# Attention with a threshold, then a maxout FFN: heads taken four at a time, and the product with v turned round

## The chip, the cores and the metric

The kernel runs on one core of one Trainium2 chip. Its time is the device time in microseconds (us); the number that counts is the median of several runs. A profiled execution of the same program gives the trace.

## The reference

For each of 8 batches and 8 heads (576 positions, 64 features a head) the scores are thresholded near the row maximum, softmaxed and multiplied with v. The heads are laid side by side to x, of 4608 rows and 512 columns, and x goes through a maxout FFN.

```python
scores = scale * np.matmul(q, k.transpose(0, 1, 3, 2))
thresh = np.max(scores, axis=-1, keepdims=True) - tau
scores = np.where(scores >= thresh, scores, -1000000000.0)
scores = scores - np.max(scores, axis=-1, keepdims=True)
attn = np.exp(scores)
attn = attn / (np.sum(attn, axis=-1, keepdims=True) + 1e-09)
x = np.matmul(attn, v)               # then heads side by side: 4608 x 512
h = np.maximum(np.maximum(x @ w1, x @ w2), x @ w3)     # 4608 x 768
out = h @ w_out
```

## The kernel before, in words

The work goes over 32 pairs of heads (8 batches, 4 pairs each). A pair is cut into 5 units of query rows: four units hold 128 rows of each of the two heads, the fifth holds the last 64 rows of both heads, stacked. A *tile* below is one 128x576 block of scores; a pair has 9 of them, a batch 36.

In a unit (`unit`), `scores` makes each tile with matmuls on half of the array: keys are split in two halves j of 288, which lie on partitions 0 to 63 and 64 to 127, so q is loaded twice, once for each half. VectorE takes the row maximum (L164). In units 0 to 2 ScalarE then makes a steep Prelu (L173) and an Exp of both heads at once (L175). In units 3 and 4 it makes one Exp (L167), and VectorE masks by comparing with a threshold (L168). P, in bf16, goes through a DMA transpose (L177) to pt. Two units later `pv_unit` multiplies: pt is the stationary operand, v with a column of ones the moving one, so the row sum comes as column 65 of the output o. `normalize` divides into X, whose rows are positions; `x_transposed` turns X by five more DMA transposes (L218) into xt. `prep` turns q and k by TensorE for the next pair, after unit 2.

The FFN of a batch is a list of 18 pieces, `todo`: the transposes of X, 12 `hid` (6 blocks of columns f by 2 parts a of the rows, 3 weights each, maximum taken by ScalarE's copy and two VectorE passes) and 5 `outp`. One piece is issued per unit, beside the attention of the next batch; the last batch's pieces follow at the end. Loads, P transposes and X transposes share SP's queue in order; v and the outputs go by POOL's queue. The engines' final order is set by the tile framework's scheduler, which may move instructions of one engine past each other where nothing forbids it.

PSUM has 8 banks: 4 for scores (two tiles), 2 for o, 2 for transposes and FFN.

Of the kernel before, what the change touches and what calls it, by code (L numbers as in the profile page):

```python
# [11 lines left out]
F32 = mybir.dt.float32  # L12
# [22 lines left out]
):  # L37
    nc = tc.nc
# [14 lines left out]


    wts = []
    for i, w in enumerate((moe_w1, moe_w2, moe_w3)):
        t = one.tile([128, 4, DF], BF16, name=f"w{i}")
        for ko in range(4):
            nc.gpsimd.dma_start(out=t[:, ko, :], in_=w[ko * 128:(ko + 1) * 128, :])
        wts.append(t)  # L60
    wo = one.tile([128, 6, DM], BF16, name="wo")
    for ko in range(6):
        nc.gpsimd.dma_start(out=wo[:, ko, :], in_=moe_w_out[ko * 128:(ko + 1) * 128, :])


    NPB = 4
    p_ring = [one.tile([128, 2, KP], BF16, name=f"pring{i}") for i in range(NPB)]
    for t in p_ring:
        nc.vector.memset(t[:, :, S:], 0.0)
    NVB = 3  # L70
    v_ring = [one.tile([128, 2, NK, D + 1], BF16, name=f"vring{i}") for i in range(NVB)]
    for t in v_ring:
        nc.vector.memset(t[:, :, :, D:], 1.0)
# [13 lines left out]
    def load(b, hp):  # L87
        h0 = 2 * hp
        qm = ld.tile([128, 2, 4, 2, D], F32, name="qm")
        ql = ld.tile([128, 2, D], F32, name="ql")  # L90
        kk = ld.tile([128, 2, 2, 2, D], F32, name="kk")
        kl = ld.tile([32, 2, 2, D], F32, name="kl")
        vt = v_ring[(b * NP + hp) % NVB]
        for i in range(2):
            h = h0 + i
            for j in range(2):
                nc.sync.dma_start(out=qm[:, i, :, j, :],
                                  in_=q[b, h, 0:512, :].rearrange("(c p) d -> p c d", p=128))
                nc.sync.dma_start(out=ql[i * 64:(i + 1) * 64, j, :], in_=q[b, h, 512:S, :])  # L99
                nc.sync.dma_start(  # L100
                    out=kk[:, i, :, j, :],
                    in_=k[b, h, j * HS:j * HS + 256, :].rearrange("(c p) d -> p c d", p=128))
            nc.sync.dma_start(
                out=kl[:, i],
                in_=k[b, h].rearrange("(j u) d -> u j d", j=2)[256:HS])
            nc.gpsimd.dma_start(out=vt[:, i, 0:4, 0:D], in_=v[b, h, 0:512, :].rearrange("(c p) d -> p c d", p=128))  # L106
            nc.gpsimd.dma_start(out=vt[0:64, i, 4, 0:D], in_=v[b, h, 512:S, :])
        return dict(b=b, hp=hp, qm=qm, ql=ql, kk=kk, kl=kl, vt=vt)

    def prep(L):  # L110

        qt = qk.tile([128, 2, 512], F32, name="qt")
        qtl = qk.tile([128, 128], F32, name="qtl")
        kt = qk.tile([128, 2, HS], F32, name="kt")
        for i in range(2):
            tp = ps_f.tile([128, 512], F32, name="tp", tag="f")
            for c in range(4):
                nc.tensor.transpose(  # L118
                    tp[:, c * 128:(c + 1) * 128],
                    L["qm"][:, i, c].rearrange("p t d -> p (t d)"),  # L120
                    identf)
            nc.scalar.activation(out=qt[:, i], in_=tp, func=AF.Copy, scale=scale)  # L122
            tk = ps_f.tile([128, 512], F32, name="tk", tag="f")
            for c in range(2):
                nc.tensor.transpose(tk[:, c * 128:(c + 1) * 128],  # L125
                                    L["kk"][:, i, c].rearrange("p j d -> p (j d)"), identf)
            nc.tensor.transpose(tk[:, 256:HS], L["kl"][:, i].rearrange("p j d -> p (j d)"), identf[:32, :32])
            if i == 1:
                nc.tensor.transpose(tk[:, 384:512], L["ql"].rearrange("p t d -> p (t d)"), identf)
                nc.vector.tensor_scalar(out=qtl, in0=tk[:, 384:512], scalar1=scale, scalar2=None, op0=OP.mult)  # L130
            nc.vector.tensor_copy(out=kt[:, i], in_=tk[:, :HS])
        L.update(qt=qt, qtl=qtl, kt=kt)
# [207 lines left out]
```

## Time and profile before

| | |
|---|---|
| median of 3 runs | 829.45 us (828.59 to 839.41) |
| the profiled execution's own time | 821.5 us |
| its span, first to last instruction | 819.7 us |
| mean granted TensorE clock | 0.872 |
| busy: TensorE (PE) | 709.2 us, 87% |
| busy: VectorE (DVE) / ScalarE (ACT) / GpSimd (POOL) | 467.7 / 410.8 / 116.6 us |
| DMA: packets, bytes | 371429, 98.49 MB |

Busy time of PE counts overlapped matmuls once and changes with the granted clock, which is 1.00 at 2.4 GHz and 0.50 at 1.2 GHz. A busy share is an average over stages that differ; the windows and the timeline tell the stages apart. The profiled execution took 0.99 of the median.

### The profile page before, as it was taken

Reading aid. Unit: us, or ns where it says so; the run is one execution under the profiler, and the core shown is the slowest. Engines: PE = TensorE matmul, PEld = TensorE weight load, DVE = VectorE, ACT = ScalarE, POOL = GpSimd, SP = SyncE. Lnnn points to the kernel's source line nnn. Section 1 sums busy time; section 2 is a strip of 40 time slices with the busy share of each in tenths; the row PEclk is TensorE's granted clock in tenths of the full one; section 3 lists DMA queues with packets and bytes.
Section 4 is the critical chain, followed back from the end, with each engine's and each line's share of the span. In section 5 each row is a group of like instructions: output and inputs, shape, how many; then the busy total and the mean of one; then the engine's idle time right before and its main releaser. Section 6 shows DMA issues by size and latency. Waiting matters only on the chain.

```text
span 819.7 us, 14313 instructions
## 1 busy us (share of the span) xinstructions
PE 709.2 (87%) x5313; PEld 427.4 (52%) x5328; DVE 467.7 (57%) x1063; ACT 410.8 (50%) x585; POOL 116.6 (14%) x192
## 2 busy tenths in 40 slices
PE   0778799987999978998899988999799997999777
PEld 0445446653566545664466644665346654666354
DVE  0467645764467645775546754675446765577432
ACT  0556534555445654566535664455545555356512
POOL 5311111101111201112101121111111121010101
PEclk9977757998589987999679995899959997899979
DMA  9989884668666667668846786676866678554611
GB/s 169 154 150 145 146 128 75 114 120 148 107 108 108 140 138 130 113 111 167 134 84 115 120 169 109 108 109 132 147 119 92 109 152 146 118 82 78 126 30 58
DMA packets 371429, 98.49 MB, mean 120 GB/s; under 512 B 366752, under 2 KB 369056, under 8 KB 371360
## 3 DMA queue, kind: packets, MB, share of 16 engines
q1 hardware_dynamic: 326912, 80.27, 53.3%
q0 software_dynamic: 44448, 17.31, 15.3%
q8 instruction: 42, 0.69, 0.3%
q14 instruction: 27, 0.22, 0.1%
HBM read 44.04 MB, written 9.44 MB: 65 GB/s over the span
## 4 chain that ended last, share of the span: by engine, by line
PE 40%; issue 25%; DMA 24%; DVE 4%; SPq 3%; ACT 2%; POOL 1%; POOLq 0%; ACTq 0%; DVEq 0%
DMA pt<-pring 15%; PE ps L140 11%; PE o L193 8%; PE ph L242 5%; PE tp L118 3%; PE po L263 3%; PE ps L146 3%; PE ph L244 3%; DMA kk<-in_k_dram 3%; DMA vring<-in_v_dram 3%; PE tk L125 2%; DMA xt<-X 2%; DVE nm L164 2%; DMA qm<-in_q_dram 1%; SPq L99 1%
## 5 line engine op out<-in xcount | busy, mean ns | idle before, releaser
L164 DVE TENSOR_REDUCE nm<-ps 128x1 f32<-128x576 f32 x288 | 216.7, 754 | 120.8 <-PE ps L140 114.4
L140 PE MATMUL ps<-kt,qt 64*128 64x288 f32 x1024 | 226.1, 502 | 5.2 <-ACT z L167 2.5
L173 ACT ACTIVATE z<-ps,bm 128x576 f32<-128x576 f32 x192 | 141.9, 739 | 110.2 <-DVE bm L172 104.0
L193 PE MATMUL o<-vring,pt 128*128 128x65 bf16 (+3 forms) x1600 | 140.2, 209 | 64.8 <-DMA pt<-pring 59.8
L193 PEld LDWEIGHTS <-pt 128*128 128x128 bf16 (+3 forms) x1600 | 98.1, 106 | 160.5 <-DMA pt<-pring 96.2
L140 PEld LDWEIGHTS ps<-kt,qt 64*128 64x128 f32 x1024 | 105.0, 211 | 60.1 <-issue 20.3
L175 ACT ACTIVATE pring<-z 128x1152 bf16<-128x1152 f32 x96 | 111.5, 1162 | 2.4
L106 POOL DMA_DIRECT2D vring<-in_v_dram x64 | 50.5, 790 | 430.6 <-PE o L193 423.9
L167 ACT ACTIVATE z<-ps,nm 128x576 f32<-128x576 f32 x96 | 70.8, 738 | 72.3 <-DVE nm L164 72.2
L249 ACT ACTIVATE hm<-ph 128x256 bf16<-128x256 f32 x96 | 39.2, 409 | 135.0 <-PE ph L246 72.1
L244 PE MATMUL ph<-xt,w 128*128 128x256 bf16 x576 | 100.1, 287 | 1.1
L242 PE MATMUL ph<-xt,w 128*128 128x256 bf16 x576 | 89.6, 299 | 11.4 <-DMA xt<-X 9.3
L251 DVE TENSOR_TENSOR hm<-ph,hm 128x256 bf16<-128x256 f32 x96 | 44.0, 458 | 87.9 <-PE ph L246 46.1
L246 PE MATMUL ph<-xt,w 128*128 128x64 bf16 x576 | 91.4, 199 | 0.7 <-DMA xt<-X 0.7
L168 DVE SCALAR_TENSOR_TENSOR pring<-z 128x576 bf16<-128x576 f32 x96 | 71.6, 752 | 14.7 <-ACT z L167 13.8
L242 PEld LDWEIGHTS <-w 128*128 128x128 bf16 x576 | 55.8, 105 | 41.2 <-DMA xt<-X 14.2
L122 ACT ACTIVATE qt<-tp 128x512 f32<-128x512 f32 x64 | 38.1, 595 | 63.9 <-PE tp L118 62.7
L244 PEld LDWEIGHTS <-w 128*128 128x128 bf16 x576 | 59.0, 102 | 20.0 <-issue 9.1
L118 PE MATMUL tp<-identf,qm 128*128 128x128 f32 x256 | 48.0, 316 | 17.6 <-DMA qm<-in_q_dram 17.6
L263 PE MATMUL po<-wo,hT 128*128 128x512 bf16 (+1 forms) x225 | 60.1, 395 | 0.8
L246 PEld LDWEIGHTS <-w 128*128 128x128 bf16 x576 | 58.2, 101 | 4.5 <-issue 2.4
L267 POOL DMA_DIRECT2D out_dram<-ob x40 | 22.5, 563 | 261.1 <-ACT ob L266 261.1
(30 smaller groups left out, 436.5 us busy)
## 6 DMA issues: line engine op xcount, KB each, us to landing
qm<-in_q_dram SPq DMA_DIRECT2D x128, 128.0 KB, 2.6
kk<-in_k_dram SPq DMA_DIRECT2D x128, 64.0 KB, 2.2
out_dram<-ob POOLq DMA_DIRECT2D x32, 256.0 KB, 2.8
vring<-in_v_dram POOLq DMA_DIRECT2D x64, 64.0 KB, 4.0
pt<-pring SPq DMA_TRANSPOSE x160, 3.5
w<-in_moe_w_dram POOLq DMA_DIRECT2D x12, 192.0 KB, 8.5
ql<-in_q_dram SPq DMA_DIRECT2D x128, 16.0 KB, 2.2
kl<-in_k_dram SPq DMA_DIRECT2D x64, 16.0 KB, 2.1
```

What stands on the lines that cost most here:

```text
L118: nc.tensor.transpose(tp[:, c * 128:(c + 1) * 128], L["qm"][:, i, c].rearrange("p t d -> p (t d)"), identf)
L140: nc.tensor.matmul(ps[:, j, :HS], L["qt"][r, i, c * 128:(c + 1) * 128], L["kt"][r, i, :], start=True, stop=True)
L164: nc.vector.tensor_reduce(out=nm, in_=pv, axis=mybir.AxisListType.XY, op=OP.max, negate=True)
L167: nc.scalar.activation(out=zi, in_=pv, func=AF.Exp, bias=nm)
L168: nc.vector.scalar_tensor_tensor(out=P[:, i, :S], in0=z[:, i], scalar=thr, in1=z[:, i], op0=OP.is_ge, op1=OP.mult)
L173: nc.scalar.activation(out=zi, in_=pv, func=AF.Prelu, bias=bm, alpha=-STEEP)
L175: nc.scalar.activation(out=P[:, 0:n, :S], in_=z[:, 0:n], func=AF.Exp)
L193: nc.tensor.matmul(dst, pt[:kr, blk + m, cols], L["vt"][:kr, i, m, :], start=(m == 0), stop=(m == NK - 1))
L242: nc.tensor.matmul(pt[:, 0:256], w, st["xt"][:, 0:2, kc, :], start=(kc == 0), stop=(kc == 3))
L244: nc.tensor.matmul(pt[:, 0:256], w, st["xt"][:, 2:4, kc, :], start=(kc == 0), stop=(kc == 3), skip_group_check=True)
L246: nc.tensor.matmul(pt[:, 256:320], w, st["xt"][:, 4, kc, :64], start=False, stop=(kc == 3), skip_group_check=True)
L263: nc.tensor.matmul(po[:r, :], st["hT"][:, f, c * 128:c * 128 + r], wo[:, f, :], start=(f == 0), stop=(f == 5))
```

## The change

Heads are taken four at a time (a *quad*, 16 in all), in 9 steps `idx` of two tiles each. Step 0 to 3 hold the first two heads, 5 to 8 the other two, step 4 the last 64 rows of all four.

- q and k are loaded once, two heads side by side, with 1 KB runs (`(p c) d`: four consecutive rows a partition). `transposed` turns a pair by 5 transposes into one tile; `qs` is a copy of q^T with its two halves of partitions swapped, by two DMAs from SBUF to SBUF on POOL's queue. Key columns are split 256 and 320.
- v is loaded in f32 by SP's queue and cast by POOL (`cast_v`).
- `softmax` does two tiles with one `bm`; the Exp is one instruction a tile and, like the masking pass, also gives the row sum (`accum_out`) into `sm`. Masked steps are 1, 4 and 7. P is 1152 wide and one DMA transpose turns it.
- `product`: v is now stationary (64 columns, a head on each half of the array's columns), pt moves, so the output is x^T at once. X, its transposes and `normalize` are gone.
- `sums`: reciprocals of the row sums are transposed, written to DRAM and read back on 64 partitions each, so `product`'s output is multiplied by rows of `rb`.
- The FFN has 17 pieces, one a step; its row parts are two of 288.
- PSUM: three slots of two banks for scores, transposes and the product, two banks for the FFN. `side` places `sums` of the quad before at step 0, its `product` at 3 and 4, and the transposes for the next quad at 5 to 8.

```diff
-    ps_s = ctx.enter_context(tc.tile_pool(name="ps_s", bufs=2, space=PSUM))
-    ps_o = ctx.enter_context(tc.tile_pool(name="ps_o", bufs=1, space=PSUM))
+    ps_s = ctx.enter_context(tc.tile_pool(name="ps_s", bufs=3, space=PSUM))
     ps_f = ctx.enter_context(tc.tile_pool(name="ps_f", bufs=2, space=PSUM))
...
+            nc.sync.dma_start(out=m, in_=src[b, h, 0:512, :].rearrange("h (p c) d -> p h c d", c=4))
+            nc.sync.dma_start(out=r, in_=src[b, h, 512:S, :].rearrange("h p d -> p h d"))
...
+    def cast_v(L):
+        vb = vp.tile([128, 4, 4, D], BF16, name="vb")
+        vrb = vp.tile([128, 2, D], BF16, name="vrb")
+        nc.gpsimd.tensor_copy(out=vb, in_=L["vm"])
+        nc.gpsimd.tensor_copy(out=vrb, in_=L["vr"])
...
+    def transposed(L, n, pr):
+        m, r = L[n + "m"], L[n + "r"]
+        ps = slot("tp")
+        h0, h1 = 2 * pr, 2 * pr + 1
+        col = 192
+        for src in (m[:, h1, 0:2], m[:, h1, 2:4], r[:, h0:h0 + 2], m[:, h0, 0:2], m[:, h0, 2:4]):
+            np_ = src.shape[0]
+            nc.tensor.transpose(ps[:, col:col + np_], src.rearrange("p a d -> p (a d)"), identf[:np_, :np_])
+            col += np_
+        t = qk.tile([128, S], F32, name=n + "t")
+        if n == "q":
+            nc.scalar.activation(out=t, in_=ps[:, 192:768], func=AF.Copy, scale=scale)
+            s = qk.tile([128, S], F32, name="qs")
+            nc.gpsimd.dma_start(out=s[0:64], in_=t[64:128])
+            nc.gpsimd.dma_start(out=s[64:128], in_=t[0:64])
+            L["qs", pr] = s
+        else:
+            nc.vector.tensor_copy(out=t, in_=ps[:, 192:768])
...
+    def softmax(L, idx, sc):
...
+        for n in range(2):
+            nc.vector.tensor_reduce(out=nm[:, n:n + 1], in_=sc[n], axis=AX, op=OP.max, negate=True)
+        if not masked:
+            bm = small.tile([128, 2], F32, name="bm")
+            nc.vector.tensor_scalar_add(bm, nm, tau)
+        for n in range(2):
+            zn = z[:, n * S:(n + 1) * S]
+            if masked:
+                nc.scalar.activation(out=zn, in_=sc[n], func=AF.Exp, bias=nm[:, n:n + 1])
+            else:
+                nc.scalar.activation(out=zn, in_=sc[n], func=AF.Prelu, bias=bm[:, n:n + 1], alpha=-STEEP)
+
+        def finish():
+            for n in range(2):
...
+                acc = sm[:, 1 - n, idx:idx + 1]
+                if masked:
+                    nc.vector.scalar_tensor_tensor(out=pn, in0=zn, scalar=thr, in1=zn,
+                                                   op0=OP.is_ge, op1=OP.mult, accum_out=acc)
+                else:
+                    nc.scalar.activation(out=pn, in_=zn, func=AF.Exp, accum_out=acc)
+            nc.sync.dma_start_transpose(out=L["pt"][:, :, idx * 128:(idx + 1) * 128], in_=P)
...
+    def sums(L):
+        rs = sp_.tile([128, 18], F32, name="rs")
+        nc.vector.reciprocal(rs, L["sm"].rearrange("p i c -> p (i c)"))
+        ps = ps_f.tile([128, 512], F32, name="rp", tag="f")
+        nc.tensor.transpose(ps[:18, 0:128], rs, identf)
...
+        nc.gpsimd.dma_start(out=rd, in_=rT)
+        rb = sp_.tile([128, W], F32, name="rb")
+        for i in range(2):
+            nc.gpsimd.dma_start(
+                out=rb[64 * i:64 * i + 64],
+                in_=rd[9 * i:9 * i + 9].rearrange("c p -> (c p)").unsqueeze(0).to_broadcast([64, W]))
...
+    def product(L, pr, xt):
+        ps = slot("o")
...
+        for a, e in halves:
+            for m in range(5):
+                for i in (1, 0):
...
+                    nc.tensor.matmul(ps[64 * i:64 * i + 64, first + a:first + e], w, x,
+                                     start=(m == 0), stop=(m == 4))
...
+            nc.vector.tensor_tensor(out=dst, in0=ps[:, first:first + S], in1=rb[:, 0:S], op=OP.mult)
...
+            fin = softmax(L, idx, sc)
+            if idx < 8:
+                sc = scores(L, idx + 1)
+            elif g + 1 < NQ:
+                sc = scores(Ls[g + 1], 0)
+            side(g, idx)
+            if todo:
+                todo.pop(0)()
+            fin()
```

Three places in the engines' order. First SP's queue where a batch's X is turned, before:

```order
L177 DMA_TRANSPOSE pt<-pring_85 128x10x128
L97 DMA qm<-in_q_dram 128x4x64
L218 DMA_TRANSPOSE xt<-X 128x4x128 x2
L177 DMA_TRANSPOSE pt<-pring_86 128x10x128
L218 DMA_TRANSPOSE xt<-X 128x4x128 x2
L218 DMA_TRANSPOSE xt<-X 128x4x64
L99 DMA ql<-in_q_dram 64x64
```

SP's queue in the middle of a batch, after the change (P is transposed to `ptq`):

```order
L194 DMA_TRANSPOSE ptq<-P 128x9x128 x5
L102 DMA vm<-in_v_dram 128x4x256
L104 DMA vr<-in_v_dram 64x2x64
L194 DMA_TRANSPOSE ptq<-P 128x9x128
L105 DMA vr<-in_v_dram 64x2x64
L194 DMA_TRANSPOSE ptq<-P 128x9x128 x2
L98 DMA qr<-in_q_dram 64x4x64
L97 DMA qm<-in_q_dram 128x4x256
```

The five transposes of X are gone from the queue, and nothing in it stands between a batch's attention and its FFN.

Second TensorE between two units of the FFN stage, before (o is the product with v, 10 such pairs a unit):

```order
L140 MATMUL ps<-kt,qt 128x288 x4
L193 LDWEIGHTS pt
L193 MATMUL o_3136<-vring_95,pt 64x65
L193 LDWEIGHTS pt
L193 MATMUL o_3136<-vring_95,pt 64x65
```

TensorE in a step with q's transposes, after (`sc` scores, `tp` transposes, `ph` FFN; each `ph` has four pairs of rows, then `w_64` and `w_65` follow):

```order
L155 MATMUL sc<-kt,qs 128x320
L155 MATMUL sc<-kt,qt 128x256
L124 MATMUL tp<-identf,qm 128x128 x2
L124 MATMUL tp<-identf,qr 128x64
L124 MATMUL tp<-identf,qm 128x128 x2
L257 LDWEIGHTS w_63
L257 MATMUL ph<-xt,w_63 128x288
L257 LDWEIGHTS w_63
L257 MATMUL ph<-xt,w_63 128x288
```

Before, the scores were followed by the product with pt; now the FFN of the step follows the scores of the next step, and the transposes stand between.

Third ScalarE in the FFN stage, before:

```order
L173 ACTIVATE z<-ps,bm 128x576
L249 ACTIVATE hm<-ph 128x256
L173 ACTIVATE z<-ps,bm 128x576
L175 ACTIVATE pring_87<-z 128x2x576
L173 ACTIVATE z<-ps,bm 128x576
L249 ACTIVATE hm<-ph 128x320
```

ScalarE there after the change (`L128` the copy of q^T, `L260` the FFN's first copy, `L182` Prelu, `L193` Exp):

```order
L128 ACTIVATE qt<-tp 128x576
L260 ACTIVATE hm<-ph 128x288
L182 ACTIVATE z<-sc,bm 128x576 x2
L193 ACTIVATE P,sm<-z 128x576 x2
L180 ACTIVATE z<-sc,nm 128x576 x2
L260 ACTIVATE hm<-ph 128x288
L128 ACTIVATE qt<-tp 128x576
```

The FFN's copy stands ahead of both Prelu passes of the step, and the Exp is two instructions.

## Rows read from the trace of the kernel before

**Rows 1.** The page: busy time by engine, and the last chain by engine.

```profile
PE 709.2 (87%) x5313; PEld 427.4 (52%) x5328; DVE 467.7 (57%) x1063; ACT 410.8 (50%) x585; POOL 116.6 (14%) x192
...
PE 40%; issue 25%; DMA 24%; DVE 4%; SPq 3%; ACT 2%; POOL 1%; POOLq 0%; ACTq 0%; DVEq 0%
```

**Rows 2.** Windows of 20 us: length, busy by engine, PEclk, DMA share, GB/s.

```profile
60.00:80.00 20.00, 18.02 (x128) 10.51 (x124) 13.49 (x30) 11.78 (x16) 2.62 (x4) 0.75 0.96 142
...
340.00:360.00 20.00, 19.07 (x177) 12.68 (x177) 15.33 (x36) 10.53 (x16) 2.62 (x4) 1.00 0.67 118
...
400.00:420.00 20.00, 18.77 (x82) 9.76 (x81) 7.42 (x16) 7.91 (x11) 1.82 (x3) 0.50 0.82 121
...
560.00:580.00 20.00, 16.66 (x138) 9.73 (x140) 11.07 (x26) 12.50 (x18) 4.67 (x8) 1.00 0.87 157
...
640.00:660.00 20.00, 19.44 (x183) 13.59 (x181) 14.29 (x34) 12.66 (x19) 2.62 (x4) 1.00 0.68 121
```

**Rows 3.** PE's timeline from 640 us, at full clock: start, us, instruction.

```profile
640.25 0.27 PE L244 MATMUL ph<-xt,w 128*128 128x256 bf16 x1
...
640.39 0.27 PE L244 MATMUL ph<-xt,w 128*128 128x256 bf16 x1
...
641.72 1.24 PE L140 MATMUL ps<-kt,qt 64*128 64x288 f32 x8
642.90 0.80 PE L193 MATMUL o<-vring,pt 128*128 128x65 bf16 x10
643.63 1.05 PE L242 MATMUL ph<-xt,w 128*128 128x256 bf16 x8
```

**Rows 4.** PE's groups in 620 to 660 us, q's transposes: busy, mean ns.

```profile
L118 PE MATMUL tp<-identf,qm 128*128 128x128 f32 x16 | 2.6, 286 | 0.0
```

**Rows 5.** Timelines at other places; last, the transposes of X over the span.

```profile
25.55 2.29 PE L140 MATMUL ps<-kt,qt 64*128 64x288 f32 x8
...
399.55 2.55 PE L140 MATMUL ps<-kt,qt 64*128 64x288 f32 x8
...
771.18 0.71 PE L146 MATMUL ps<-kt,qtl 64*64 64x288 f32 x8
...
778.84 6.41 SPq L218 DMA_TRANSPOSE xt<-X  x5
...
808.16 6.75 PE L263 MATMUL po<-wo,hT 128*128 128x512 bf16 x29
...
L218 SPq DMA_TRANSPOSE xt<-X x40: 1188/1260/1683, 105.0 to 784.1; - x40
```

**Rows 6.** Groups of DVE, ACT and POOL over the span, by form.

```profile
L164 DVE TENSOR_REDUCE nm<-ps 128x1 f32<-128x576 f32 x288 | 216.7, 754 | 120.8 <-PE ps L140 114.4 <-PE ps L146 3.8
L173 ACT ACTIVATE z<-ps,bm 128x576 f32<-128x576 f32 x192 | 141.9, 739 | 110.2 <-DVE bm L172 104.0 <-PE o L193 1.6
...
L175 ACT ACTIVATE pring<-z 128x1152 bf16<-128x1152 f32 x96 | 111.5, 1162 | 2.4
...
L168 DVE SCALAR_TENSOR_TENSOR pring<-z 128x576 bf16<-128x576 f32 x96 | 71.6, 752 | 14.7 <-ACT z L167 13.8
L167 ACT ACTIVATE z<-ps,nm 128x576 f32<-128x576 f32 x96 | 70.8, 738 | 72.3 <-DVE nm L164 72.2
...
L251 DVE TENSOR_TENSOR hm<-ph,hm 128x320 bf16<-128x320 f32 x48 | 23.6, 492 | 47.7 <-PE ph L246 46.1 <-ACT hm L249 1.2
...
L249 ACT ACTIVATE hm<-ph 128x320 bf16<-128x320 f32 x48 | 20.9, 435 | 72.9 <-PE ph L246 72.1
...
masks.py:199 POOL TENSOR_SCALAR_AFFINE_SELECT identf<-identf 128x128 f32<-128x128 f32 x1 | 0.3, 304 | 0.1
```

**Rows 7.** A DMA queue, time of P's transposes to landing, and the wait for them.

```profile
q1 hardware_dynamic: 326912, 80.27, 53.3%
...
pt<-pring SPq DMA_TRANSPOSE x160, 3.5
...
PEld L193 <- DMA pt<-pring: 96.2, 65, 4.1
```

More of the change, by code (lines that the diff above doesn't have):

```diff
@@ L52 @@
     make_identity(nc, identf)
[L55 to L73, printed above, removed]
+    wts = [one.tile([128, 4, DF], BF16, name=f"w{i}") for i in range(3)]
+    wo = one.tile([128, NF, DM], BF16, name="wo")
+    def weight_loads():
+        for i, w in enumerate((moe_w1, moe_w2, moe_w3)):
+            yield lambda i=i, w=w: nc.gpsimd.dma_start(
+                out=wts[i], in_=w.rearrange("(ko p) f -> p ko f", p=128))
+        yield lambda: nc.gpsimd.dma_start(
+            out=wo, in_=moe_w_out.rearrange("(ko p) f -> p ko f", p=128))
@@ L110, in prep @@
[L110 to L132, printed above, removed]
@@ L270, in ffn_pieces @@
         return pieces
+    quads = [(b, qd) for b in range(B) for qd in range(H // 4)]
+    NQ = len(quads)
+    Ls = [None] * (NQ + 1)
+    xts = {}
     todo = []
[L274 to L287 removed]
@@ L289, with side @@
-    for n, (b, hp) in enumerate(pairs):
-        if hp == 0:
-            X = xp.tile([128, 5, DM], BF16, name="X")
-        Ln = load(*pairs[n + 1]) if n + 1 < len(pairs) else None
-        for c in range(5):
-            pt = unit(L, c)
-            waiting.append((L, c, pt, X))
-            drain(2)
+    prep = [("q", 0), ("k", 0), ("q", 1), ("k", 1)]
+    def side(g, idx):
+        if g + 1 < NQ and 5 <= idx <= 8:
+            transposed(Ls[g + 1], *prep[idx - 5])
+        if g > 0:
+            if idx == 0:
+                sums(Ls[g - 1])
+            elif idx in (3, 4):
+                b, qd = quads[g - 1]
+                if b not in xts:
+                    xts[b] = xp.tile([128, 4, S], BF16, name="xt")
+                product(Ls[g - 1], idx - 3, xts[b])
+                if idx == 4 and qd == 1:
+                    todo.extend(ffn(b, xts[b]))
@@ new lines @@
+    wl = list(weight_loads())
+    Ls[0] = load(*quads[0])
+    for a in prep:
+        transposed(Ls[0], *a)
+    cast_v(Ls[0])
+    sc = scores(Ls[0], 0)
+    for g in range(NQ):
+        L = Ls[g]
+        L["sm"] = sp_.tile([128, 2, 9], F32, name="sm")
+        L["pt"] = pt_pool.tile([128, 9, W], BF16, name="ptq")
+        for idx in range(9):
+            if idx == 0 and g + 1 < NQ:
+                Ls[g + 1] = load(*quads[g + 1])
+            if idx == 2 and g + 1 < NQ:
+                cast_v(Ls[g + 1])
+            fin = softmax(L, idx, sc)
[4 more added lines that the diff above has]
+            side(g, idx)
@@ L297 @@
             if todo:
                 todo.pop(0)()
-            if c == 2 and Ln is not None:
-                prep(Ln)
-        L = Ln
-    drain(0)
+            fin()
+            if wl and idx >= 2:
+                wl.pop(0)()
+    while todo:
+        todo.pop(0)()
+    side(NQ, 0)
+    side(NQ, 3)
+    side(NQ, 4)
     while todo:
```

268 lines of the change are left out of this document (112 added, 156 removed).

## The prediction

> **What bounds the kernel now.** I read the page first: TensorE is busy 87% of the span and no other engine over 57%, and in the chain that ended last PE holds 40% and DMA 24% [rows 1]. So TensorE is the engine to follow, but not alone. The windows tell two stages apart [rows 2]. From 640 us, with FFN pieces beside the attention, PE is busy 19.4 of 20 us at a granted clock of 1.00: TensorE sets the time there. From 400 us, where a batch's X is turned, the clock is 0.50 and 20 us hold 82 matmuls in place of 183. In the first batch, without FFN (60 to 80 us), the clock is 0.75 and the DMA engines are 0.96 busy.
>
> How much is lost outside the good stage follows from one batch. At full clock [rows 3 to 5]: two tiles of scores take 1.24 us and a tile of the stacked unit 0.71, so 16 x 1.24 + 4 x 0.71 = 22.7 us; the product with v 20 x 0.80 = 16.0; `hid` with 256 columns 1.05 us for 8 matmuls, 72 of them 9.5; the 256 and 64 columns of the other half start every 0.14 us (two starts between 640.25 and 640.39), 72 of them 10.1; `outp` 6.75 us for 29, 30 of them 7.0; 60 transposes at 2.6 / 16 = 0.16 us, 9.8. The sum is 75 us. But a batch takes (778.84 - 105.0) / 7 = 96.3 us from one turning of X to the next [rows 5]. So 21 us a batch go to waits for P's transposes (PEld alone waited 96.2 us for them, 65 times [rows 7]), to the turning of X, and to the low clock that follows.
>
> **The change, part by part, for one batch.** TensorE at full clock:
>
> - Scores: as many tiles. Rows of the array take 256 and 320 columns in turn, which evens out over two tiles: 22.7 us. If each tile waited for its 320 columns it would be 1.24 x 320/288 = 1.38 a pair, 2.2 us more.
> - Transposes: 40, and 2 small ones for the sums: 42 x 0.16 = 6.8 us, 3 less.
> - Product: 80 matmuls of 288 columns on average. The trace has no such matmul. By the column rate above (320 columns in 0.14 us) one is 0.126 us. If the two halves of the array's columns work side by side that is 5.0 us, if in turn 10.1. A stacked tile is four matmuls on quarters of the array and takes 0.71 us, where two on half the array take 0.62 [rows 3, 5]: the halves do work side by side, so I take 5.0.
> - `hid`: 144 matmuls of 288 columns, 18.1 us, 1.5 less. `outp`: 7.0.
>
> The sum is 60 us (65 if the halves take turns), 15 less than before.
>
> ScalarE: 410.8 / 8 = 51.4 us a batch now. 12 wide Exps of 1.162 us become 24 of half the width that also give the sum. One is at least half, 0.58, and at most the 0.739 of a pass of that width [rows 6]; I take 0.70, nearer to the pass, since a pass has a fixed part: 12 x (1.40 - 1.16) = 2.9 more, 54. VectorE: 58.5 a batch now; the maxima, masks and reduces stay, `normalize` and the small tiles of q go, x^T's four passes come (at most 0.75 each by L164), so 56 to 59. The mask's row sum may add up to the 0.30 us of the smallest pass shown, 12 of them 3.6. All three engines have 54 to 60 us to do in a batch, and the time hangs on how they interlock.
>
> Waits that come. Each step's scores need slots of PSUM that the Prelu (or Exp) of the step before frees, and ScalarE's order has the FFN's copy of the step ahead of it. I follow four kinds of step, with 0.1 us for a hand-over as an estimate:
>
> - q or k transposes and `hid` (6 a batch): 5 x 0.16 + 0.65 until the first weight's result, copy 0.435, two Prelu of 0.74, the second tile of scores 0.62, four hand-overs: 4.3 us; TensorE has 1.24 + 0.8 + 1.51 = 3.55 to do. Loss 0.74 x 6 = 4.4.
> - masked steps beside `hid` or alone (4 a batch that count): VectorE does two reduces, two masks and two maxima, 1.5 + 1.5 + 1.0 + 0.3 = 4.3 us, against 2.75 to 3.55. Loss about 3.8.
> - plain steps (4): ScalarE needs 1.48 + 1.40 + 0.44 + 0.2 = 3.5 against 2.75. Loss 3.0.
> - product steps (4): the third slot is held until VectorE has read it, about 0.5 each. Loss 2.0.
>
> That is 13 us; with 2 for the row sums, a batch is 60 + 15 = 75 us, TensorE 80% busy. At 83% (16.66 of 20 us, 560 to 580 us) the granted clock was 1.00 [rows 2], so I reckon with the full clock.
>
> Edits at nothing: the product comes three steps, some 12 us, after its quad's last P, so the 3.5 us of a P transpose [rows 7] is covered, and so is the chain of the sums (two transfers of that order one after the other, some 8 us). If the steps were shorter than 3 us this cover would go. On POOL's queue the copies into `qs` stand behind casts, loads of weights and outputs; they have three steps as well. The turning of X, 6.41 us and a cold clock each time [rows 5], goes, and nothing takes its place: the FFN's input is a VectorE pass away from the product. DMA: 144 x 1152 packets for P, 24,576 of 1 KB and 12,288 of 256 B for q, k, v, some 11,000 large ones for swaps, sums and output, about 214,000 in place of 371,429. q1's 326,912 packets took 53% of the engines [rows 7], so I expect less than before.
>
> **The sum.** Start: the first scores came at 25.55 us [rows 5]. The swaps again stand behind weights on POOL's queue: 25. Then 22 steps without FFN (the first batch is complete at step 4 of the third quad), at a low clock as in the first batch now: half of 2.55 for a tile of scores [rows 5], reduce 0.75, Prelu 0.74, 0.55 for the small pass and hand-overs make 3.3 us, and 11 of them have a side piece of 1.1: 85. Then 122 steps, 18 a batch: 6.78 x 75 = 508. The end, now 819.7 - 778.84 = 41 us, begins with the sums and the last product: 46. Together 664 us; with the 1.8 us that lie around the span 666; the median stands at 829.45 / 821.5 = 1.01 of the profiled execution, so 672 us.
>
> **The rivals.**
>
> - *TensorE stays filled.* The scheduler moves the FFN's matmuls between scores; if it hides all four losses, a batch is 62 and the whole 664 - 6.78 x 13 = 576, 584 as a median. For it: PE at 19.4 of 20 now, with the same two buffers for the FFN. Against: ScalarE and VectorE had slack then. 12%.
> - *The column halves take turns.* 5.1 us a batch more: 707. For it: no row shows moving operands of two halves at 128 rows. 9%.
> - *The cast holds VectorE.* POOL now reads and writes 128x1024 a quad. By its 0.304 us for 128x128 a cast is 2.4 us, by VectorE's 0.49 us for 320 columns 1.6. If VectorE's mask, which reads z twice from SBUF, stood still for it, 16 x 2.4 = 38 us: 711. No run shows POOL at work beside VectorE. 6%. The Trainium skill has it as a rule: by "SBUF — State Buffer", section "SBUF: two separate sides", GpSimd and a VectorE instruction with two inputs from SBUF want one shared pair of ports, and whoever has it blocks the other for the whole instruction. No run here shows it.
> - *DMA bound by bytes.* Bytes rise to 105 MB (P 42.5, q, k, v 28.3, swaps, sums and output 9.4 each, weights 6). At 60 to 80 us 142 GB/s filled the engines to 0.96 [rows 2]: 740 us, 780 with the end. Against: these were packets of 256 B nearly all, and now most bytes beyond P's come in larger ones. 8%.
> - *Slower: the clock stays low.* Each step waits for ScalarE or VectorE, and if that is enough to drop the clock as at 400 us, where it was 0.50, two tiles take 2.55 in place of 1.24, and 60 us of work become 120. With the clock low throughout: 25 + 110 + 6.78 x 120 + 50 = 1000 us. A batch may take 97 us before the gain is gone; at 80% busy that is 78 us of TensorE work, reached when 30% of it runs at the low clock. Against: 560 to 580 us. 7%. The Trainium skill ("TensorE: Matmul & The Clock Gate", Part 1) calls the low rate the default, released by activity; the trace agrees, its 0.50 windows follow waits.
>
> **How the numbers follow.** The forecast has 58%; its own range is 625 to 715, from three quarters of the losses hidden to a fifth more of all. The range 590 to 775 takes in both middle rivals and halves of the first and of the DMA case, and leaves out some 17%. Faster by over 2% (about what can be told from no change here): all but the last and a little of the DMA case, 0.92; within 2% 0.02; slower 0.06.
>
> **What would show it.** Granted clock 1.00 in the middle and PE about 80% busy there; a batch every 75 us; no turning of X, and products that don't wait for P's transposes; PE's total near 500 to 560 us. Wrong if: the clock is below 0.85 in the middle; Exps with the sum cost over 0.9 us; ten products of a half take 2.5 us in place of 1.3; DVE's mask grows beside a cast; or scores wait over 1 us a step for their slot.

## The result and the profile after

The changed kernel takes 648.21 us (median of four runs, 647.39 to 653.27) against 829.02 us of the kernel before in the same comparison (824.27 to 839.41): a ratio of 0.785, 95% interval 0.780 to 0.790. Forecast were 672 us, 590 to 775. The profiled execution took 653.27 us, with a span of 651.5 us and a mean granted clock of 0.982 (0.872 before).

The page of the changed kernel: busy time by engine, the queue q1 that carries P's transposes, and the last chain by engine, against [rows 1, 7].

```profile
PE 568.4 (87%) x3634; PEld 311.4 (48%) x3648; DVE 423.1 (65%) x880; ACT 389.8 (60%) x841; POOL 105.3 (16%) x194
...
q1 hardware_dynamic: 209152, 70.80, 54.7%
...
PE 43%; ACT 24%; DVE 17%; issue 7%; DMA 6%; POOL 0%; SPq 0%; ACTq 0%; POOLq 0%; DVEq 0%
```

PE's share of the span is 87% in both kernels, and tells nothing of the change. Its busy time fell by 141 us, and the chain's make-up changed: DMA 6% in place of 24%, time without a named cause ("issue") 7% in place of 25%, ScalarE and VectorE 41% in place of 6%. q1 has 36% fewer packets and holds the engines for the same share of a shorter span.

Windows of the changed kernel, against [rows 2] (length, busy by engine, PEclk, DMA share, GB/s); the second is a whole batch:

```profile
60.00:80.00 20.00, 16.77 (x60) 8.99 (x56) 12.87 (x26) 10.45 (x22) 3.11 (x7) 1.00 0.67 154
313.90:385.30 71.40, 67.45 (x456) 37.28 (x456) 52.81 (x111) 48.24 (x105) 12.69 (x23) 1.00 0.82 175
400.00:420.00 20.00, 18.20 (x135) 10.00 (x128) 14.46 (x29) 12.38 (x27) 2.86 (x5) 1.00 0.72 170
560.00:580.00 20.00, 18.97 (x122) 11.09 (x121) 16.64 (x38) 13.29 (x31) 2.61 (x5) 1.00 0.66 119
```

There is no window at 0.50 in the middle any more. In a batch TensorE is busy 67.5 of 71.4 us, which is 94% and not the 80% of the forecast. From 400 and from 560 us VectorE and ScalarE do more in 20 us than before.

How long a batch takes is read from its first `outp` matmul to that of the next. These are the starts, from the last chain of the changed kernel (start, us, what):

```profile
171.48 1.03 PE po L268 x4
...
242.88 1.03 PE po L268 x4
...
314.28 1.03 PE po L268 x4
...
385.75 1.03 PE po L268 x4
...
457.15 1.03 PE po L268 x4
```

A batch is 71.4 us, the same four times over (the next one took 72.9, so that the table below has a mean of 71.8); 75 was forecast, and before it was 96.3. Inside one batch the chain changes hands. From 350 us in the same view:

```profile
350.38 1.26 ACT z L182 x2
351.64 1.33 ACT P L193 x4
...
353.26 0.61 DVE nm L173
...
355.28 0.73 ACT z L182
356.01 1.32 ACT P L193 x4
...
363.19 1.32 ACT P L193 x4
...
365.51 1.13 PE sc L160 x16
366.64 1.70 PE o L232 x20
368.35 1.09 PE ph L257 x8
...
371.26 1.70 PE o L232 x20
```

From 350 to 364.8 us the batch runs on ScalarE and VectorE (maximum, bias, Prelu, Exp), and then on TensorE without a gap: scores, both products of a quad, `hid`. The chain's pieces between 313.9 and 385.3 us add up to 33 us on PE, 20 on ScalarE, 13 on VectorE and 5.5 without a named cause. So the chain doesn't stay on the engine that is busiest: the engines wait for one another in turn, in a ring.

The groups that the change brought (busy, mean ns, idle before), where [rows 6] has those of before:

```profile
L193 ACT ACTIVATE P<-z 128x576 bf16<-128x576 f32 x192 | 130.0, 690 | 0.0
...
L190 DVE SCALAR_TENSOR_TENSOR P<-z 128x576 bf16<-128x576 f32 x96 | 71.4, 753 | 24.8 <-ACT z L180 24.8
...
L112 POOL CAST vb<-vm 128x1024 bf16<-128x1024 f32 x16 | 16.7, 1042 | 145.6 <-issue 114.9
L193 ACT ACTIVATION_READ_ACCUMULATOR P<-z 128x1 f32 x192 | 40.0, 208 | 0.0
```

The Exp of half the width takes 0.69 us, and an instruction of its own of 0.21 us reads the sum; these follow the Exp closely, and two Exps with their reads take 1.33 us on the chain (351.64). I reckoned with 1.40.

The start and the end, in the changed kernel's timeline (start, us, instruction, idle time before it and who ended it):

```profile
16.02 1.54 POOL L68 DMA_DIRECT2D w<-in_moe_w_dram  x2
17.55 0.55 POOL L130 DMA_DIRECT2D qs<-qt  x1
...
32.58 3.03 PE L155 MATMUL sc<-kt,qs 64*128 64x256 f32 x6 [13.13 <-DMA qs<-qt]
...
603.66 0.27 DVE L200 RECIPROCAL rs<-sm 128x18 f32<-128x18 f32 x1 [3.80 <-ACT P L193]
...
606.44 0.52 POOL L206 DMA_DIRECT2D rd<-rT  x1 [0.85 <-DVE rT L204]
...
609.04 1.04 POOL L209 DMA_DIRECT2D rb<-rd  x2 [1.54 <-DMA rd<-rT]
...
614.34 0.76 DVE L237 TENSOR_TENSOR xt<-o,rb 128x576 bf16<-128x576 f32 x1 [8.19 <-DMA rb<-rd]
...
615.15 1.37 PE L257 MATMUL ph<-xt,w 128*128 128x288 bf16 x4 [5.32 <-DVE xt L237]
```

The first scores that use the swapped copies of q wait 13 us for them; the copies are issued on POOL's queue right behind two loads of weights. At the end the row sums need 10.7 us from the reciprocal to the multiplication, and TensorE stands idle for 5.3 of them.

### The profile page after: what moved, and what is told of

Same layout as the page of the kernel before. It is cut to its first block, busy times and chain, and to the rows that moved or that the text cites. A ratio compares the mean times of both kernels' runs of the same rounds, so it can differ in the third digit from the quotient of the medians.

```text
span 651.5 us, 10435 instructions
## 1 busy us (share of the span) xinstructions
PE 568.4 (87%) x3634; PEld 311.4 (48%) x3648; DVE 423.1 (65%) x880; ACT 389.8 (60%) x841; POOL 105.3 (16%) x194
## 2 busy tenths in 40 slices
DMA packets 220661, 103.09 MB, mean 158 GB/s; under 512 B 187184, under 2 KB 214208, under 8 KB 220608
## 4 chain that ended last, share of the span: by engine, by line
PE 43%; ACT 24%; DVE 17%; issue 7%; DMA 6%; POOL 0%; SPq 0%; ACTq 0%; POOLq 0%; DVEq 0%
PE sc L155 15%; PE ph L257 13%; ACT P L193 8%; ACT z L182 8%; DVE nm L173 8%; PE tp L124 7%; PE o L232 5%; DVE P L190 4%; DMA qs<-qt 2%; PE po L268 2%; ACT z L180 2%; DMA rb<-rd 2%; ACT qt L128 2%; ACT ob L271 2%; DMA vm<-in_v_dram 2%
## 5 line engine op out<-in xcount | busy, mean ns | idle before, releaser
L173 DVE TENSOR_REDUCE nm<-sc 128x1 f32<-128x576 f32 x288 | 208.6, 752 | 100.3 <-PE sc L155 82.3
L155 PE MATMUL sc<-kt,qs 64*128 64x256 f32 (+1 forms) x512 | 188.9, 473 | 39.4 <-ACT z L182 22.6
L182 ACT ACTIVATE z<-sc,bm 128x576 f32<-128x576 f32 x192 | 134.0, 742 | 122.5 <-DVE bm L176 105.7
L257 PE MATMUL ph<-xt,w 128*128 128x288 bf16 x1152 | 178.1, 289 | 15.2 <-DVE xt L237 5.3
L155 PE MATMUL sc<-kt,qt 64*128 64x256 f32 (+1 forms) x512 | 181.8, 467 | 5.0 <-ACT qt L128 3.0
L193 ACT ACTIVATE P<-z 128x576 bf16<-128x576 f32 x192 | 130.0, 690 | 0.0
L155 PEld LDWEIGHTS sc<-kt,qs 64*128 64x128 f32 x512 | 84.6, 197 | 72.9 <-ACT z L182 38.7
L155 PEld LDWEIGHTS sc<-kt,qt 64*128 64x128 f32 x512 | 86.4, 197 | 45.8 <-issue 22.2
L190 DVE SCALAR_TENSOR_TENSOR P<-z 128x576 bf16<-128x576 f32 x96 | 71.4, 753 | 24.8 <-ACT z L180 24.8
L128 ACT ACTIVATE qt<-tp 128x576 f32<-128x576 f32 x32 | 20.8, 651 | 79.8 <-PE tp L124 79.8
L260 ACT ACTIVATE hm<-ph 128x288 bf16<-128x288 f32 x96 | 39.7, 413 | 47.6 <-PE ph L257 47.6
L180 ACT ACTIVATE z<-sc,nm 128x576 f32<-128x576 f32 x96 | 67.2, 751 | 0.0
L193 ACT ACTIVATION_READ_ACCUMULATOR P<-z 128x1 f32 x192 | 40.0, 208 | 0.0
## 6 DMA issues: line engine op xcount, KB each, us to landing
w<-in_moe_w_dram POOLq DMA_DIRECT2D x3, 768.0 KB, 10.8
```

Source lines behind the costliest of these rows:

```text
L155: nc.tensor.matmul(ps[:, cols], t[rows, off:off + 128], L["kt", pr][rows, kc], start=True, stop=True)
L173: nc.vector.tensor_reduce(out=nm[:, n:n + 1], in_=sc[n], axis=AX, op=OP.max, negate=True)
L180: nc.scalar.activation(out=zn, in_=sc[n], func=AF.Exp, bias=nm[:, n:n + 1])
L182: nc.scalar.activation(out=zn, in_=sc[n], func=AF.Prelu, bias=bm[:, n:n + 1], alpha=-STEEP)
L190: nc.vector.scalar_tensor_tensor(out=pn, in0=zn, scalar=thr, in1=zn, op0=OP.is_ge, op1=OP.mult, accum_out=acc)
L193: nc.scalar.activation(out=pn, in_=zn, func=AF.Exp, accum_out=acc)
```

## The experiments

Theory after the result: of the 181 us about half were waits (P's transposes, X's turning, the low clock that follows), and the rest is TensorE's smaller work, on which a batch now rests together with the hand-overs between the engines. Rival: one of the two alone explains it. All medians, with the ratio to the kernel before on the same chip and the mean length of a batch (from the second first `outp` to the sixth, in the trace):

| kernel | us | ratio (95% interval) | a batch, us |
|---|---|---|---|
| before | 829.02 | 1 | 96.3 |
| `b_lateffn` | 802.58 | 0.974 (0.966 to 0.982) | 93.2 |
| `b_lateprod` | 753.02 | 0.914 (0.907 to 0.922) | 87.8 |
| `b_both` | 746.81 | 0.906 (0.898 to 0.914) | 85.5 |
| `b_lessprod` | 736.55 | 0.898 (0.890 to 0.906) | 83.7 |
| `a_twoslots` | 745.10 | 0.905 (0.895 to 0.914) | 82.9 |
| `a_turns` | 694.58 | 0.842 (0.834 to 0.850) | 76.4 |
| `a_early` | 678.29 | 0.823 (0.815 to 0.831) | 75.4 |
| after | 648.21 | 0.785 (0.780 to 0.790) | 71.8 |
| `a_best` | 647.83 | 0.787 (0.781 to 0.793) | 71.7 |
| `a_noaccum` | 646.00 | 0.784 (0.777 to 0.790) | 70.2 |
| `a_splitbm` | 644.48 | 0.781 (0.772 to 0.789) | 71.8 |
| `a_swap` | 640.73 | 0.776 (0.769 to 0.784) | 71.4 |
| `a_lesshid` | 636.21 | 0.775 (0.770 to 0.780) | 69.6 |

Names with `b_` are edits of the kernel before, with `a_` of the changed one.

**`a_turns`: the two halves of the array in turn.**

```diff
-            for m in range(5):
-                for i in (1, 0):
+            for i in (1, 0):
+                for m in range(5):
```

> Changed kernel, but each half of the product runs all its five matmuls for one head before the other head, so the two column halves of the array can't work side by side. If they do work side by side now (ten matmuls in 0.85 us), ten in turn take 1.3 to 1.5 us, 64 times 0.45 to 0.65 us: 29 to 42 us more TensorE work, of which steps that wait anyway hide up to half: 15 to 42 us slower than the changed kernel. If the halves take turns already: no change, within 4 us.

It is 46 us slower than the changed kernel, a little over the range given. The product's largest group shows it; from the changed kernel's groups by shape:

```profile
L232 PE MATMUL o<-ptq,vb 128*64 128x288 bf16 x256 | 23.8, 311 | 2.0 <-ACT z L182 2.0
```

and with the halves in turn:

```profile
L232 PE MATMUL o<-ptq,vb 128*64 128x288 bf16 x256 | 46.1, 306 | 2.0 <-ACT z L182 2.0
```

One matmul lasts the same, but their union is twice as long: matmuls for the two halves of the columns overlap if they are issued in alternation, and don't if five of one half come first. Over all six shapes the product goes from 66 to 129 us, 8 a batch. Of the 63 us, 46 are seen in the time, 5.0 in each batch. Most of TensorE's work in this place is on the path.

**`a_early`: the product two steps earlier.**

```diff
-            elif idx in (3, 4):
+            elif idx in (1, 2):
...
-                product(Ls[g - 1], idx - 3, xts[b])
-                if idx == 4 and qd == 1:
+                product(Ls[g - 1], idx - 1, xts[b])
+                if idx == 2 and qd == 1:
```

> Changed kernel with the product two steps earlier (steps 1 and 2 after its quad in place of 3 and 4). The chain of the sums takes some 12 us from the reciprocal to the landed broadcast, three steps of 4 us. If that cover is needed, VectorE and the slot wait 3 to 6 us a quad: 40 to 100 us slower, with VectorE's x^T pass waiting for the broadcast. If the cover is not needed: within 5 us.

30 us slower, less than the 40 that I gave as the least, but far from nothing; the clock is 0.937. The waits of VectorE and TensorE (total, times, longest):

```profile
DVE xt L237 <- DMA rb<-rd: 37.7, 11, 9.1
...
PE ph L257 <- DVE xt L237: 12.1, 6, 5.6
```

In the changed kernel the first of them is 9.7 us in two times, nearly all of it the 8.19 us at the end. So the three steps do cover the chain of the sums, and with one step it lies open: VectorE waits, and with it all that is queued behind it. P's transposes need little of that cover: in this whole run the product's weight loads wait 2.9 us for them and its matmuls 1.7.

**`a_noaccum`: without the reads of the Exp's sum.**

```diff
-                    nc.scalar.activation(out=pn, in_=zn, func=AF.Exp, accum_out=acc)
+                    nc.scalar.activation(out=pn, in_=zn, func=AF.Exp)
...
+        nc.gpsimd.memset(L["sm"], 1.0)
```

> Changed kernel without the row sums of the six unmasked steps (they are set to 1; the output is not divided there). It removes 192 reads of the accumulator of 0.21 us, of which about 0.1 overlaps the next pass. If hand-overs between ScalarE, VectorE and TensorE set the middle stage: 8 to 25 us faster. If TensorE's work alone sets it: within 3 us.

2.2 us, within what the rival gave; a batch is 1.2 us shorter. ScalarE's busy time fell by 17 us and not by the 40 of the reads: more than half of the reads' time lies over the passes beside them. My theory that the hand-overs on ScalarE are worth 8 to 25 us fell here; that TensorE's work alone sets the middle, as the rival has it, doesn't follow, as `a_lesshid` shows below.

**`a_swap`: the first quad's swapped copies on SP's queue.**

```diff
-            nc.gpsimd.dma_start(out=s[0:64], in_=t[64:128])
-            nc.gpsimd.dma_start(out=s[64:128], in_=t[0:64])
+            eng = nc.sync if (L["b"], L["qd"]) == (0, 0) else nc.gpsimd
+            eng.dma_start(out=s[0:64], in_=t[64:128])
+            eng.dma_start(out=s[64:128], in_=t[0:64])
```

> Changed kernel, with the first quad's four copies into qs on SP's queue instead of POOL's, where they stand behind three loads of weights. If that queue is what held the first scores for 13.1 us: 10 to 13 us faster than the changed kernel. If the DMA engines themselves are full of weights then, the copies land as late as now: 0 to 3 us.

7.5 us faster than the changed kernel (637.17 to 643.48 against 647.39 to 653.27), less than the 10 to 13 that I gave. The wait that was 13.13 us is gone, all but this (line numbers one higher):

```profile
PE sc L156 <- DMA qs<-qt: 2.3, 1, 2.3
```

The first maximum starts 10.6 us earlier, and a batch stays at 71.4 us. The start is the one place where I found something to win; `a_best` below doesn't keep it.

**`b_lateprod`: the kernel before, its product two units later.**

```diff
-    NPB = 4
+    NPB = 6
...
-    NVB = 3
+    NVB = 4
...
-    pt_pool = ctx.enter_context(tc.tile_pool(name="pt", bufs=4))
+    pt_pool = ctx.enter_context(tc.tile_pool(name="pt", bufs=6))
...
-            drain(2)
+            drain(4)
```

> This is the kernel before with its product two units later (four units after the softmax in place of two; six buffers for pt and for P, four for v), so that P's transposes have more time. Theory (about 21 us a batch of the kernel before went to waits for P's transposes, to the turning of X and to the low clock, and their going is most of the gain): the 96 us that the weight loads waited for pt all but go; 20 to 60 us faster, 770 to 810, and the middle windows at a granted clock nearer to 1.00. Rival (the gain is the smaller work of TensorE, 15 us a batch of the 24, and the waits are covered by other engines anyway): 0 to 10 us faster.

72 us faster, more than I gave it. The wait of the weight loads for pt, 96.2 us in [rows 7]:

```profile
PEld L193 <- DMA pt<-pring: 41.6, 27, 3.0
```

The edit also gives v's ring a fourth buffer. TensorE's matmuls waited 4.7 us for v's loads in the kernel before, and that part of the 72 us is not told apart here.

**`b_lateffn`: the kernel before, two empty pieces behind the turning of X.**

```diff
         pieces.append(tr)
+        pieces.append(lambda: None)
+        pieces.append(lambda: None)
```

> This is the kernel before with two empty pieces in the FFN's list behind the turning of X, so that the first hid stands two units later and X's transposes have landed by then. Theory: the stretch around 400 us no longer waits with the clock at 0.50 and the seven turnings of X give back 3 to 7 us each: 20 to 50 us faster, 780 to 810. Rival (X's transposes cost by being in SP's queue ahead of P's, not by what waits for X): 0 to 10 us faster, and the weight loads' wait for pt stays near 96 us.

22 us faster; the wait for pt is 103.5 us, not less. So what waits for X costs some 20 us, and P's transposes are a cost of their own. The low clock is not X's alone either. In the kernel before, around the turning at 400 us (a window, TensorE, SP's queue):

```profile
395.00:400.00 5.00, 4.62 (x30) 3.00 (x32) 2.65 (x9) 2.67 (x4) 0.82 (x2) 0.50 0.51 107
...
395.38 1.07 PE L193 MATMUL o<-vring,pt 128*128 128x65 bf16 x10 [2.27 <-DMA pt<-pring]
...
400.34 1.20 SPq L218 DMA_TRANSPOSE xt<-X  x1
```

The granted clock is at 0.50 by the end of a wait for pt, some 5 us before the first transpose of X is issued. At six of the seven turnings from 210 us on it has fallen before that transpose.

**`b_both`: both edits.**

> The kernel before with both edits: the product two units later, and two empty pieces behind the turning of X. Theory: with both waits gone the kernel before comes to what its own work of TensorE wants, some 75 us a batch plus its hand-overs: 50 to 110 us faster, 720 to 780, with the clock at 1.00 in most windows. Rival (smaller work of TensorE): within 15 us of the kernel before.

78 us faster. The two edits overlap: 72 and 22 alone, 78 together. The trace of this kernel, in the batch from 358.5 us (windows as above):

```profile
358.50:443.50 85.00, 80.98 (x665) 50.54 (x666) 57.98 (x133) 50.63 (x73) 13.20 (x22) 0.96 0.81 140
```

PE is busy 95% of the batch at a clock of 0.96, and of the last chain's pieces listed there, 83 us, 71 are PE's. So with most of these waits gone TensorE is busy nearly throughout, at 85.5 us a batch. What is left to the changed kernel, 14 us, is about what PE's busy time shrank by from there: 81.0 to 67.5 us a batch. That the one causes the other isn't shown by this; the next run tests it.

**`b_lessprod`: `b_both` with two fifths of the product.**

```diff
-            for m in range(NK):
+            for m in range(2):
                 kr = 128 if m < 4 else 64
                 nc.tensor.matmul(dst, pt[:kr, blk + m, cols], L["vt"][:kr, i, m, :],
-                                 start=(m == 0), stop=(m == NK - 1))
+                                 start=(m == 0), stop=(m == 1))
...
-            nc.vector.reciprocal(rs[:, :n], ov[:, :, 64])
+            nc.vector.reciprocal(rs[:, :n], ones5[:, :n])
```

> The kernel before with both edits (product two units later, two empty pieces behind the turning of X), and its product over 2 of the 5 blocks of keys in place of 5, with the row sums replaced by one: three fifths of the product are left out. That leaves 80 matmuls with their weight loads a batch, at 0.08 us each 6.4 us, as much as the ten-pair product of the changed kernel takes (6.8). Theory (what still lies between the kernel before without its waits, 747, and the changed kernel, 648, is the product's time on TensorE): 8 x 9.6 = 77 us shorter, shown to 70% or more, 667 to 695. Rival (the other half comes from fewer transposes, VectorE's normalize or P's packets): within 25 us of 747, 722 or more.

10 us. My theory that the product's time alone is the rest fell. Where a part of it went is seen at the turn of a batch, in the windows of this kernel:

```profile
365.20:381.70 16.50, 11.57 (x65) 6.22 (x65) 8.73 (x24) 7.94 (x12) 1.58 (x3) 0.69 0.89 137
381.70:391.70 10.00, 9.96 (x81) 6.41 (x79) 7.11 (x14) 5.10 (x8) 0.00 (x0) 1.00 0.61 126
```

and in its timeline, SP's queue and TensorE:

```profile
366.57 6.45 SPq L221 DMA_TRANSPOSE xt<-X  x5
...
369.54 0.40 PE L193 MATMUL o<-vring,pt 128*128 128x65 bf16 x4 [2.65 <-DMA pt<-pring]
...
373.12 1.22 SPq L177 DMA_TRANSPOSE pt<-pring  x1
...
375.74 0.26 PE L193 MATMUL o<-vring,pt 128*64 128x65 bf16 x4 [1.34 <-DMA pt<-pring]
...
378.66 0.40 PE L249 MATMUL ph<-xt,w 128*128 128x256 bf16 x1
```

Five transposes of X hold the queue for 6.45 us, the next of P starts only at 373.12, TensorE waits for pt, and the `hid` that follows runs at 0.40 us a matmul in place of 0.27. The weight loads' wait for pt is 61.3 us here, against 29.9 in `b_both`: what TensorE no longer does, it waits. In the batch from 345.2 us it is idle 8.5 us, 4.9 of them in the first of these windows, against 4.0 us in the whole batch of `b_both`.

**`a_twoslots`: the changed kernel with two slots of PSUM in place of three.**

```diff
-    ps_s = ctx.enter_context(tc.tile_pool(name="ps_s", bufs=3, space=PSUM))
+    ps_s = ctx.enter_context(tc.tile_pool(name="ps_s", bufs=2, space=PSUM))
```

> The changed kernel with two slots of PSUM in place of three for scores, transposes and the product (the kernel before had two for scores, its product and transposes apart). Theory (in a good part of a batch the step is a ring of scores, maxima, Prelu and Exp over ScalarE and VectorE, and the third slot is what lets TensorE do the side pieces meanwhile): the batch goes from 71.4 to 80 to 95 us, 715 to 830 us in all, with the granted clock below 1.00 in the middle. Rival (TensorE is full and its own work alone sets the batch, so that a slot less only changes the order): up to 3 us a batch, 648 to 675.

97 us slower than the changed kernel; VectorE's wait for scores grew from 82.3 to this:

```profile
DVE nm L173 <- PE sc L155: 139.4, 107, 15.1
```

So with a ring that is too tight the changed kernel comes to 745 us, no better than `b_both`, for all the smaller work of TensorE. It is a harsher test than the layout of the kernel before, whose product and transposes had banks of their own.

**`a_lesshid`: three quarters of `hid`.**

```diff
-                for kc in range(4):
+                for kc in range(3):
...
-                                     start=(kc == 0), stop=(kc == 3))
+                                     start=(kc == 0), stop=(kc == 2))
```

> The changed kernel with three of the four blocks of x's columns in hid: a quarter of the FFN's first product is left out, 36 matmuls of 288 columns a batch, 4.5 us each batch by 0.126 us, 36 us in all. Theory (TensorE's own work sets the middle stage and the end): 60 to 100% of it is given back, 22 to 36 us, 612 to 627. Rival (the hand-overs between the engines set the step, as in my sum of the prediction, where the losses were of ScalarE and VectorE): 3 to 12 us, mostly at the end, 636 to 645.

12 us, where 36 us of matmuls were left out: a third shown, 1.8 of 4.5 us in a batch. TensorE alone doesn't set the middle. Against `a_turns` (5.0 of 8 us a batch) it suggests where it does: in the steps with the product, which run without a gap from 364.9 us on, and less in the others.

**`a_splitbm` and `a_best`.** The first gives each of a step's two tiles its own maximum and bias; the second adds `a_swap` and takes the last quad's transfers of the sums to SP's queue.

```diff
-            nc.vector.tensor_reduce(out=nm[:, n:n + 1], in_=sc[n], axis=AX, op=OP.max, negate=True)
-        if not masked:
-            bm = small.tile([128, 2], F32, name="bm")
-            nc.vector.tensor_scalar_add(bm, nm, tau)
+            nm = small.tile([128, 1], F32, name=f"nm{n}")
+            nc.vector.tensor_reduce(out=nm, in_=sc[n], axis=AX, op=OP.max, negate=True)
+            nms.append(nm)
+            if not masked:
+                bm = small.tile([128, 1], F32, name=f"bm{n}")
+                nc.vector.tensor_scalar_add(bm, nm, tau)
+                bms.append(bm)
```

> The changed kernel with the maximum's column, and the bias made from it, apart for each of a step's two tiles, so that the first Prelu can start after the first reduce and not after the second. Theory that the hand-overs of a step cost what my sum gave them: 5 to 20 us faster than the changed kernel (628 to 643). Rival (TensorE's own work sets the middle stage): within 3 us, 645 to 651.

> The changed kernel with the first quad's swapped copies on SP's queue, the maximum and bias apart for each of a step's tiles, and for the last quad the two transfers of the row sums on SP's queue. By the runs so far 7.5 and 3.7 us, and 1 to 3 us at the end: 634 to 640. Rival (the two edits meet the same wait for the first scores, and the transfer of the sums is no shorter from SP): 640 to 645.

`a_splitbm`: 3.7 us, with ranges that overlap (641.41 to 652.52), and a batch of 71.8 us; an earlier first Prelu is worth nothing in the ring. It is worth something where no FFN runs beside the attention: in its trace 62 us pass from the first maximum to the first `hid`, against 73 in the changed kernel, and the next batch gives 5 of them back (76.5 us). `a_best` was a miss: 647.83 us, no better than the changed kernel. Its first `outp` starts at 154.5 us, 16.6 earlier, but its batches take 71.6 to 75.8 us, and at the end VectorE waits for `rb` as long from SP's queue as from POOL's:

```profile
605.32 0.76 DVE L242 TENSOR_TENSOR xt<-o,rb 128x576 bf16<-128x576 f32 x1 [8.21 <-DMA rb<-rd]
```

In the trace, its fastest execution, the first `outp` comes 7.6 us earlier than in `a_swap`, and the batches that start at 154.5 and 516.9 us lose 4.4 and 3.5 of that, each with the granted clock at 0.66 for 5 us. What brings these on is open.

## Why the prediction was right, step by step

- **The sum.** 25 + 85 + 508 + 46 us were forecast; measured in the span are 34.8 to the first maximum, 73 to the first `hid`, 492 for the 122 steps, 52 for the end. The start was too short by 10: I had seen the swaps behind the weights and priced that at nothing, though first scores at 25.55 us [rows 5] didn't have the 13 us wait in them. The 22 steps were too long by 12: I put them at the low clock, and at 60 to 80 us it was 1.00. But in `a_swap`, where it was 0.74 there, they took 73 us too, so that clock didn't set them; `a_splitbm` took 62, so the hand-over from the maxima to the Prelu did in part. The steps with FFN were 16 too long and the end 6 too short. So part of this cancelled. The factor of 1.01 from the profiled execution to the median was the wrong way: it is 0.99 here, which makes about half of the 24 us between forecast and measurement.
- **The batch.** 75 forecast, 71.4 measured, and that they are so near is in part luck. I had 60 us of TensorE's work and 15 us of losses, TensorE 80% busy; measured are 67.5 us busy and 3.9 idle. The work was too low by 7.5 us, the idle time too high by 11. By groups, scores are busy 27.4 us (22.7 in the sum) and `hid` 22.0 (18.1), and the product is 6.8 and not 5.0, as ten matmuls on each half take 1.70 us (366.64 in the chain), 0.17 a pair where I took 0.126 from the rate of `hid`. Busy time isn't TensorE at its peak, so some of the 7.5 us may be waiting inside the pieces; the runs don't tell. That TensorE doesn't set the batch alone is shown by the chain, half of it on ScalarE and VectorE, and by `a_lesshid`; the losses by kind of step were only argued, and 13 us of idle time did not come. ScalarE and VectorE have less to do than I had, 48.2 and 52.8 us in place of 54 and 56 to 59, and the sums' extra cost on ScalarE, 2.9 us a batch in the sum, shows as 1.2 in the time (`a_noaccum`).
- **21 us a batch of waits before.** `b_both` gives back 10.8. Of the other 10, some 6 were my count of TensorE's work, too low: its rows add up to 75 us, but in `b_both` PE is busy 81 at a clock of 0.96; 4 are idle time that is left there. The difference to the changed kernel, 15, was nearly right (81.0 to 67.5), as the same rows were summed on both sides. That the low clock follows the turning of X was misread: it mostly falls before it (`b_lateffn`).
- **The halves side by side.** Right, by `a_turns`: in turn the product's work grows by 8 us a batch (I had 5.1), and 5.0 of it show.
- **Edits at nothing.** Three steps cover the chain of the sums, as `a_early` shows by taking two of them away; P's transposes need little of them. The turning of X is gone, and nothing took its place.
- **Rivals.** TensorE filled (584 us) had the busy share nearer than I did (94% of a batch), but lies too low: PE's busy time is 67.5 us, where this rival's whole batch has 62. DMA by bytes (103.09 MB, 220661 packets) bound nothing in the middle: the windows are at 0.66 to 0.82. The clock didn't stay low. The cast didn't hold the masks, 753 ns against 752 before, but none ran beside one in this trace; where one did, in `a_swap`, it took 1.58 us (shown below). So the rival's mechanism is there, and here the engines' order kept it from showing. The cast itself took 1.04 us and not 2.4.
- **What would make it wrong.** Of the signs that I named, the clock was 1.00 in the middle, an Exp with its read at most 0.90, and the ten matmuls on each half 1.70 us, between 1.3 and 2.5 and nearer to the first. Of the signs that it is right two failed: PE was 94% busy in a batch and not 80%, and its total is 568 us, above 500 to 560.

So of the 181 us 78 are shown to go with waits that two small edits take out of the kernel before. For the other 103 these runs speak for the smaller work of TensorE and the looser ring (18 steps for 20 units, a third slot) together: a smaller product alone gave 10 us (`b_lessprod`), and without the third slot 97 are lost again (`a_twoslots`). That no third part of the change, such as the `normalize` and the transposes that went, has a share isn't shown. How the 103 divide can't be told from these runs.

## What to carry to other kernels

Take out the waits in the old layout first, by moving the consumer a unit or two later: here that costs a few buffers and shows 43% of what the rewrite brought. When one engine's work is cut, look for the ring that is just behind it, by reading the chain inside one period and not its share of the span; here a smaller product in the old layout was mostly waited away. A sum that comes out near the measured time isn't thereby right: here too little work and too much idle time made up for each other. A transfer in a queue that others share is priced by who stands behind it: X's turning held the queue for 6.45 us in `b_lessprod`, with P's next transpose behind it, and the swaps of the first quad came 13 us late behind weights that nobody needed yet, of which moving them won 7.5.

## What the runs showed of the hardware

A cast on POOL holds a VectorE instruction that is 2 elements wide. The timeline of the changed kernel, first the bias with no cast beside it, then with one:

```profile
325.05 0.17 DVE L176 TENSOR_SCALAR bm<-nm 128x2 f32<-128x2 f32 x1
...
335.38 1.04 POOL L112 CAST vb<-vm 128x1024 bf16<-128x1024 f32 x1 [4.94 <-issue]
335.69 0.75 DVE L176 TENSOR_SCALAR bm<-nm 128x2 f32<-128x2 f32 x1
...
336.54 1.37 ACT L182 ACTIVATE z<-sc,bm 128x576 f32<-128x576 f32 x2 [3.73 <-DVE bm L176]
```

The add takes 0.75 us in place of 0.17 and ends at 336.44, with the cast (335.38 + 1.04 = 336.42), and both Prelu wait for it. It happens five times, every second quad from the one at 192.58 us on: under 3 us in all. The reduces from PSUM and the products with `rb` beside a cast keep their length (0.68 for L241), and so do the adds of `a_splitbm`, which are 1 element wide (0.15). A mask, which reads z twice from SBUF, is held too, in `a_swap`:

```profile
40.87 1.04 POOL L112 CAST vb<-vm 128x1024 bf16<-128x1024 f32 x1 [14.06 <-DMA vm<-in_v_dram]
40.94 1.58 DVE L191 SCALAR_TENSOR_TENSOR P<-z 128x576 bf16<-128x576 f32 x1
```

It ends 0.61 us after the cast and takes 0.83 us longer than the usual 0.75; in `a_twoslots` one beside a cast takes 1.40. The Trainium skill, "SBUF — State Buffer", section "SBUF: two separate sides", has a pair of ports that GpSimd and some VectorE instructions lock for a whole instruction; the ends of the add and of the mask agree with that. Whether this add is of the kind that the page names, no run here shows.

Two matmuls on halves of the array's columns, 128 rows each, take 0.17 us a pair of 288 columns if they alternate (1.70 us for ten pairs) and 0.34 if not (3.4 us on `a_turns`' chain). An accumulator's read is an instruction of its own: 208 ns on ScalarE, of which about 115 lie over the Exp that it follows, and 83 ns on VectorE.
